# Attention scores over 64-key half-blocks in 32x64 tiles, with a vector-engine mask on the strip that both halves share

## The chip, the cores and the metric

The kernel runs on one core of one Trainium2 chip. Times are device microseconds (us) of that core. Kernels are compared only within the same rounds. The engines are called by the profile's names: PE (TensorE; PEld is its weight load), DVE (VectorE), ACT (ScalarE), POOL (GpSimd) and SP (SyncE).

## The reference, cut to what matters

```python
xn = layernorm(x)                                  # x: 2048 tokens x 512, bf16
qkv = xn @ wqkv                                    # 32 heads of 16
scores = q @ k.T * 16 ** -0.5                      # per head
mask = (i - j >= 0) & (i - j < 256)                # causal, a window of 256 keys
o = softmax(where(mask, scores, -1e9)) @ v
B = ((xn @ w_gate) * (xn @ w_up)) @ w_down         # 512 -> 1792 -> 512, no activation
return x + o @ wo + B
```

The kernel works on four chunks T of 512 tokens. Dense matmuls (projections, gate, up, down, output projection) are "fillers", which it places between the small matmuls of the attention.

## The kernel before

A head pair of one chunk needs, for its 512 queries, keys from 256 tokens back. Before, keys come in blocks of 128. Scores are made transposed (keys on partitions, queries on columns), four heads at a time in four 32-row tiles of PE. A block of 128 keys is met by 384 queries, and of its three 128x128 squares the outer two are triangles that are masked by POOL after the exponential. Three batches of 512 columns hold one parity of the heads:

```python
GROUPS = (                                         # (key block, first q, last q, column)
    ((-2, 0, 0, 0), (0, 0, 2, 128)),
    ((-1, 0, 1, 0), (2, 2, 3, 256)),
    ((1, 1, 3, 0), (3, 3, 3, 384)),
)
def scores(self, T, c, par, i):
    S = self.ps_s.tile([128, 4, 512], F32, tag="S", name="S")
    for kb, q0, q1, col in parts:
        for e in range(4):                         # 4 row tiles, 4 PSUM banks
            nc.tensor.matmul(S[:, e, col:col + n], lhsT=K[32*e: ..., 128 keys],
                             rhs=Q[...], tile_position=(32 * e, 0), ...)      # L223
    nc.scalar.activation(out=P[...], in_=S[...], func=ACT.Exp, scale=0.25)    # L231
    # one affine_select of 128x512 on POOL for each triangle                  # L236, L240
def values(self, T, c, par):                       # two batches later
    for i in range(3):
        for kb, q0, q1, col in self.parts(T, i):
            for e in range(4):                     # 4 column tiles of 17 rows
                nc.tensor.matmul(acc[32*e:32*e+17, ...], lhsT=V[..., 0:17],
                                 rhs=P[:, e, ...], tile_position=(0, 32 * e)) # L256
    # DVE: transpose, reciprocal; then divide(): a product, and a transpose to OT
```

A score batch is one piece of a loop: scores, then (when a pair is complete) the value block of two batches ago, then fillers. `fill` stops at a filler whose `after` has not been reached; the output projection `wo` has one, because it needs OT of its chunk. Three PSUM buffers serve all fillers; DVE empties most of them.

The softmax here doesn't subtract the row's maximum and nothing guards it: scores larger than these inputs give would overflow.

## Time and profile before

| | before |
|---|---|
| time, median of 3 runs (with a fourth, taken later: 279.87) | 279.71 us (279.6 to 280.08) |
| PE, DVE, ACT, POOL busy, of a span of 277.8 us | 269.4, 188.1, 183.1, 164.3 us |
| chain of work that ended last | 89% PE |
| PE instructions in the program | 4830 |

These lines are from the page of the kernel before: part 1 (busy time and share of the span), DVE's row of part 2 (busy tenths in 40 slices of the span), and part 4 (the chain).

```profile
## 1 busy us (share of the span) xinstructions
PE 269.4 (97%) x2396; PEld 115.0 (41%) x2414; DVE 188.1 (68%) x338; ACT 183.1 (66%) x121; POOL 164.3 (59%) x284
...
DVE  6388989788567777858855778774853477777232
...
PE 89%; ACT 5%; DVE 3%; issue 1%; DMA 1%; POOL 0%; ACTq 0%
```

PE is the limit: it is busy for 97% of the span, and the chain is nearly all PE.

The next lines are groups of part 5 (line, engine, operation, output<-input, count | busy us, mean ns of one | idle time before, and what ended it).

```profile
L231 ACT ACTIVATE P<-S 128x2048 bf16<-128x2048 f32 (+2 forms) x96 | 170.0, 1771 | 74.3 <-PE S L223 62.6
L236 POOL TENSOR_SCALAR_AFFINE_SELECT P<-P 128x512 bf16<-128x512 bf16 x128 | 84.7, 662 | 54.3 <-ACT P L231 54.1
...
L256 PE MATMUL accb<-P,V 128*17 128x384 bf16 (+2 forms) x704 | 25.3, 276 | 0.0
```

The exponential (L231) is 96 times up to 1.88 us; POOL's selects (L236 and L240) are 240 times 0.65 us. Both have idle time of tens of us that costs nothing. The 704 score and 704 value matmuls are the PE part of attention.

The timeline of PE near 101 us (start us, duration us, engine, line, operation, and the count that was merged) shows one burst:

```profile
101.36 0.40 PE L223 MATMUL S<-Q,K 16*128 16x256 bf16 x8
101.68 0.83 PE L256 MATMUL accb<-P,V 128*17 128x128 bf16 x24
102.45 0.39 PE L289 MATMUL gp<-xnT,Wg 128*128 128x512 bf16 x1
```

Eight score matmuls take 0.32 us to the start of the next thing, though they have 512 columns in each row tile, and 24 value matmuls take 0.77 us for 1536 columns in each column tile. A 512-column filler matmul starts every 0.216 us, so 1536 columns at full rate are 0.65 us.

### The profile page before, as it was taken

The numbers are of one execution on the slowest core, as the hardware profiler recorded it, in microseconds if no ns is written. First come the engines' busy times: TensorE is split into PE (matmuls) and PEld (weight loads), VectorE is DVE, ScalarE is ACT, GpSimd is POOL, SyncE is SP. The second block draws the span as 40 slices with busy tenths as digits, with TensorE's granted clock in tenths as the row PEclk, the third lists the DMA queues.
The fourth block names the chain that finished last, engine by engine and source line by source line (L and its number), as shares of the span: only waits on it lengthen the run. The fifth ranks groups of instructions, "written<-read, shape, count | busy, mean of one in ns | idle before, by whom it ended". The sixth has DMA issues, their size and how long they took to land.

```text
span 277.8 us, 5829 instructions
## 1 busy us (share of the span) xinstructions
PE 269.4 (97%) x2396; PEld 115.0 (41%) x2414; DVE 188.1 (68%) x338; ACT 183.1 (66%) x121; POOL 164.3 (59%) x284
## 2 busy tenths in 40 slices
PE   7999999999999999999999999999999999999994
PEld 6433433433344434343444344444434444433453
DVE  6388989788567777858855778774853477777232
ACT  3666766786767666688666676769676766767601
POOL 4146666765786656574777656575656566656510
PEclk9999999999999999999999999999999999999999
DMA  6999511000111100000012200000001000000002
GB/s 211 377 371 348 113 21 21 19 2 0 39 40 57 21 2 0 1 2 0 2 40 61 53 2 2 0 2 1 0 2 40 19 21 1 2 0 2 0 2 76
DMA packets 17163, 13.74 MB, mean 49 GB/s; under 512 B 7025, under 2 KB 17137, under 8 KB 17137
## 3 DMA queue, kind: packets, MB, share of 16 engines
q1 hardware_dynamic: 16848, 13.18, 15.6%
q8 instruction: 19, 0.31, 0.5%
q10 hardware_dynamic: 288, 0.20, 0.2%
q14 instruction: 8, 0.06, 0.1%
HBM read 9.70 MB, written 2.10 MB: 42 GB/s over the span
## 4 chain that ended last, share of the span: by engine, by line
PE 89%; ACT 5%; DVE 3%; issue 1%; DMA 1%; POOL 0%; ACTq 0%
PE up L300 18%; PE gp L289 18%; PE psd L317 18%; PE S L223 11%; PE qkp L177 9%; PE accb L256 8%; PE psd L323 5%; ACT P L231 3%; PE vp L165 3%; ACT V L169 1%; DMA x<-in_A_x_dram 1%; DVE st L116 1%; DVE hT L304 0%; DVE gsb L294 0%; PE xTp L151 0%
## 5 line engine op out<-in xcount | busy, mean ns | idle before, releaser
L231 ACT ACTIVATE P<-S 128x2048 bf16<-128x2048 f32 (+2 forms) x96 | 170.0, 1771 | 74.3 <-PE S L223 62.6
L236 POOL TENSOR_SCALAR_AFFINE_SELECT P<-P 128x512 bf16<-128x512 bf16 x128 | 84.7, 662 | 54.3 <-ACT P L231 54.1
L240 POOL TENSOR_SCALAR_AFFINE_SELECT P<-P 128x512 bf16<-128x512 bf16 x112 | 72.5, 647 | 38.4 <-ACT P L231 38.4
L300 PE MATMUL up<-xnT,Wu 128*128 128x512 bf16 x224 | 60.0, 380 | 0.1
L289 PE MATMUL gp<-xnT,Wg 128*128 128x512 bf16 x224 | 59.7, 380 | 0.0
L317 PE MATMUL psd<-Wd,hT 128*128 128x512 bf16 (+1 forms) x225 | 52.3, 366 | 1.4 <-issue 1.1
L263 DVE STREAM_TRANSPOSE at<-accb 128x512 f32<-128x512 f32 x32 | 22.8, 713 | 39.0 <-PE accb L256 39.0
L304 DVE TENSOR_TENSOR hT<-up,gsb 128x512 bf16<-128x512 f32 x56 | 38.1, 680 | 7.8 <-PE up L300 5.8
L294 DVE CAST gsb<-gp 128x512 bf16<-128x512 f32 x56 | 37.9, 676 | 5.9 <-PE gp L289 5.8
L317 PEld LDWEIGHTS <-hT 128*128 128x128 bf16 x238 | 21.5, 98 | 24.9 <-issue 4.7
L289 PEld LDWEIGHTS <-Wg 128*128 128x128 bf16 x224 | 20.0, 98 | 26.1 <-issue 5.2
L177 PE MATMUL qkp<-xnT,Wqkv 128*128 128x512 bf16 x128 | 30.6, 380 | 0.0
L300 PEld LDWEIGHTS <-Wu 128*128 128x128 bf16 x224 | 19.6, 98 | 26.4 <-issue 7.0
L256 PE MATMUL accb<-P,V 128*17 128x384 bf16 (+2 forms) x704 | 25.3, 276 | 0.0
L341 DVE TENSOR_TENSOR y<-psd,x 128x512 bf16<-128x512 f32 (+1 forms) x15 | 9.9, 666 | 17.9 <-PE psd L323 16.5
L223 PE MATMUL S<-Q,K 16*128 16x256 bf16 (+2 forms) x352 | 18.4, 276 | 0.5
L223 PE MATMUL S<-Q,Ko 32*128 32x256 bf16 (+2 forms) x352 | 18.4, 275 | 0.5 <-ACT P L231 0.2
L276 DVE TENSOR_TENSOR on<-at,rz 128x256 bf16<-128x256 f32 x32 | 18.1, 565 | 0.4
L177 PEld LDWEIGHTS <-Wqkv 128*128 128x128 bf16 x128 | 11.4, 98 | 14.6 <-issue 2.7
L256 PEld LDWEIGHTS <-V 128*17 128x17 bf16 x704 | 13.8, 90 | 8.7 <-issue 5.3
L182 DVE CAST K<-qkp 128x512 bf16<-128x512 f32 x16 | 11.0, 688 | 8.9 <-PE qkp L177 8.6
L323 PE MATMUL psd<-Wo,OT 128*128 128x512 bf16 (+1 forms) x67 | 16.6, 367 | 0.2 <-issue 0.2
(39 smaller groups left out, 141.1 us busy)
## 6 DMA issues: line engine op xcount, KB each, us to landing
Wg<-in_B_w_gate_dram SPq DMA_DIRECT2D x2, 896.0 KB, 10.1
Wu<-in_B_w_up_dram SPq DMA_DIRECT2D x2, 896.0 KB, 11.6
Wd<-in_B_w_down_dram SPq DMA_DIRECT2D x1, 1792.0 KB, 15.9
out_dram<-y SPq DMA_DIRECT2D x14, 128.0 KB, 1.7
Wqkv<-in_A_wqkv_dram SPq DMA_DIRECT2D x3, 512.0 KB, 5.5
x<-in_A_x_dram SPq DMA_DIRECT2D x1, 1024.0 KB, 10.5
x<-in_A_x_dram SPq DMA_DIRECT2D x1, 512.0 KB, 10.9
Wo<-in_A_wo_dram SPq DMA_DIRECT2D x1, 512.0 KB, 15.9
```

The costliest lines, as they stand in the source:

```text
L177: nc.tensor.matmul(ps[:], lhsT=self.Wqkv[:, k, lo:lo + 128], rhs=self.xnT[T][:, :, k, :], start=(k == 0), stop=(k == 3))
L223: nc.tensor.matmul(S[:, e, col:col + n], lhsT=(self.Ko if par else self.K)[U][rows, c, 128 * j:128 * j + 128], rhs=self.Q[T][rows, c, 128 ...
L231: nc.scalar.activation(out=P[:, :, lo:hi], in_=S[:, :, lo:hi], func=ACT.Exp, scale=0.25)
L236: nc.gpsimd.affine_select(out=P[:, :, j:j + 128], in_=P[:, :, j:j + 128], pattern=[[0, 4], [1, 128]], compare_op=ALU.is_ge, fill=0.0, base ...
L240: nc.gpsimd.affine_select(out=P[:, :, j:j + 128], in_=P[:, :, j:j + 128], pattern=[[0, 4], [-1, 128]], compare_op=ALU.is_gt, fill=0.0, bas ...
L256: nc.tensor.matmul(acc[32 * e:32 * e + 17, 128 * q0:128 * q0 + n], lhsT=self.V[U][:, v, 8 * c + 2 * e + par, 0:17], rhs=P[:, e, col:col + ...
L289: nc.tensor.matmul(ps[:], lhsT=self.Wg[:, k, 128 * f:128 * f + 128], rhs=self.xnT[T][:, :, k, :], start=(k == 0), stop=(k == 3))
L294: nc.vector.tensor_copy(out=self.gsb[:], in_=ps[:])
L300: nc.tensor.matmul(ps[:], lhsT=self.Wu[:, k, 128 * f:128 * f + 128], rhs=self.xnT[T][:, :, k, :], start=(k == 0), stop=(k == 3))
L304: nc.vector.tensor_tensor(out=self.hT[T][:, f, :], in0=ps[:], in1=self.gsb[:], op=ALU.mult)
L317: nc.tensor.matmul(ps, lhsT=self.hT[T][:, f, 128 * b:128 * b + 128], rhs=self.Wd[:, f, c0:c1], start=(f == 0), stop=False)
L323: self.nc.tensor.matmul(ps, lhsT=self.OT[T][:, c, 128 * b:128 * b + 128], rhs=self.Wo[:, c, c0:c1], start=False, stop=(c == 3))
```

## The change

The intent: cut keys in halves of 64. A half-block is met by 320 queries, not 384, so fewer columns lie outside the window. Score tiles become 32 rows by 64 columns of PE: the two halves of a block sit side by side in the array and give the partitions 0-63 and 64-127 of the same columns. The five batches EVEN, ODD, PLAIN, EVEN, ODD then do for a head pair (both parities) what six did; in the first chunk four do. Of the eight 64-column strips of an EVEN or ODD batch, six need a mask (five in the first chunk; PLAIN needs none). Four (three in the first chunk) are masked by POOL selects of half the old size. The other two are shared: there half 0 and half 1 belong to different key blocks and queries. Their value matmuls read a copy of V in which the other half's rows are zero (Vu, Vl0, Vl1), and their two different masks are put on by DVE, as a minimum with a constant tile. This instruction is placed at the end of the batch, behind its fillers, so that DVE does not stand waiting for the exponential. The pace of the loop changed too: fillers are now shared out evenly over the batches, and no longer by the columns of each batch.

```diff
-        self.work = pool("work", 3)
+        self.work = pool("work", 2)
-        self.ypool = pool("ypool", 5)
+        self.ypool = pool("ypool", 4)
+        self.diag = const.tile([128, 3, 64], BF16, name="diag")          # mask: BIG or 0
...
+    def zero_halves(self, j):
+        for h in (0, 1) if j == 0 else (1,):
+            self.nc.gpsimd.memset(self.Vh[j][h][64 - 64 * h:128 - 64 * h], 0.0)
+    def copy_halves(self, T):
+        for h in range(2):
+            rows = slice(64 * h, 64 * h + 64)
+            self.nc.vector.tensor_copy(out=self.Vh[T % 2][h][rows], in_=self.V[T][rows])
...
+        self.zero_halves(0)                                    # in first_chunk
...
+    def batches(self, T):
+        if T == 0:
+            return [(EVEN, 0), (ODD, 0), (EVEN, 1), (ODD, 1)]
+        return [(EVEN, 0), (ODD, 0), (PLAIN, None), (EVEN, 1), (ODD, 1)]
...
+        return first + second + [                              # of score_pieces: half 0 and 1
+            (par, J, 0, q, 320, 64), (par, J, 1, q + 64, 320, 128),
+            (par, J + 2, 0, q + 256, 128, 384), (par, J + 2, 1, q + 320, 64, 448)]
...
-                nc.tensor.matmul(S[:, e, col:col + n], ... tile_position=(32 * e, 0),
+                nc.tensor.matmul(S[outs, e, col:col + n], ... tile_position=(32 * e, outs.start),
...
-        nc.scalar.activation(out=P[:, :, lo:hi], in_=S[:, :, lo:hi], func=ACT.Exp, scale=0.25)
+        nc.scalar.activation(out=P[:], in_=S[:], func=ACT.Exp, scale=0.25)
...                                                             # selects of 64 columns, 4 per batch
+    def mask_shared(self, T, c, kind, par):
+        if kind == PLAIN:
+            return
+        P = self.strips[(T, c, kind, par)]
+        both = P.rearrange("p e (b x) -> p e b x", x=64)[:, :, 1:7:5, :]
+        m = self.diag[:, 0:2, :] if T == 0 else self.diag[:, 1:3, :]
+        self.nc.vector.tensor_tensor(out=both, in0=both, op=ALU.min,
+                                     in1=m.unsqueeze(1).to_broadcast([128, 4, 2, 64]))
...
+        return first + [(64, 0, J, q, 64), (128, 2, J, q + 64, 256), (384, 1, J, q + 320, 64),
+                        (384, 0, J + 2, q + 256, 64), (448, 2, J + 2, q + 320, 64)]   # value_pieces
...
+            V = self.V[U] if h == 2 else self.Vh[U % 2][h]      # in values
...
             if values(g - LAG):
                 fill(min(spent + 4, upto), g)
                 divide(g - LAG)
+                T, c, par = due[g - LAG]
+                if (c, par) == (3, 1):
+                    self.copy_halves(T + 1)
-            fill(upto, g)
+            if g < len(steps) - 1:
+                fill(upto, g)
+                self.mask_shared(*s)
```

## The prediction

> **What bounds it.** TensorE. Page part 1: PE busy 269.4 of 277.8 us (97%), DVE 188.1, ACT 183.1, POOL 164.3; the chain that ended last is 89% PE; no wait of PE for an engine is over 1.4 us in total (waits). So only PE time counts, unless the change starves PE.
>
> **PE, read from the timeline.** 512-column matmuls start 0.216 us apart. A tiled burst costs its columns plus about 0.1 us of turn-around on each side: one score batch (8 matmuls, 4 row tiles together) runs 101.36-101.68, though 512 columns need 0.213; a value block (24 matmuls, 4 column tiles) 101.68-102.45. In it each piece costs its columns and 3 to 7 ns more.
>
> **Removed.** 96 batches become 76 (12x5 for T>0, 16 for T=0): about 20x0.43 = 8.6 us of PE; ACT 20 fewer exponentials of up to 1.88 us, about -28 us; POOL keeps 240 selects at half the size (about 0.4 us for 0.65, an estimate between the 293 ns at 128 elements and 647 at 512): -60 us. ACT and POOL are off the chain: worth nothing.
>
> **Added.** PE instructions 4830 -> 9438: score matmuls 704 -> 1792, value matmuls 704 -> 1920, each with a weight load. Value columns stay 1536 per head, but in 16 pieces for 6; at 5 ns more each that is +0.05 us x 24, +1.5 us in all. A head pair (T>0) costs now 4x0.43+2x1.19 = 4.1 us, then about 5x0.45+2x0.83 = 3.9 (both 64-key halves side by side, 512 columns): with everything ideal the PE gains only 3 to 4 us, 1.3%.
>
> DVE gains 64 masks (two SBUF inputs, 512 bf16; I estimate 0.45 to 0.65 us from Ko 440 ns and xn 552) and 8 copies of 2304 elements (about 1 us): +35 to 50 us, to 225-240. In gate/up stretches (85-123) DVE is already 76% busy and frees three PSUM buffers; it goes over 90% there, costing PE 1 to 5 us.
>
> **Main doubt: instruction issue.** Now the longest burst is 8+24 matmuls, 64 instructions with loads, in 1.1 us. The new one is 24+64, 176 instructions, with array work for only 1.1 to 1.2 us. The Trainium skill ("TensorE: Matmul & The Clock Gate", table at its head) gives a 64-deep PE queue: today's burst just fits and no gap shows inside it, so the trace does not reveal the sequencer's rate. "Runtime: NRT & Kernel Launch", Instruction fetch mechanics, gives an issue floor of about 20 cycles; at the 1.2 GHz that the TensorE page states that is 17 ns. An estimate from these: 112 unqueued instructions take 1.9 us, 0.7 us over, x24, plus 0.5 x 8 at T=0: about +20 us. At 10 ns it costs nothing; at 28 ns +58.
>
> **Prediction.** -4 (PE work) +2 (DVE) +10 (issue, weighted) = 288 us; range 271 to 320. Faster by over 2% 0.13, within 2% 0.26, slower 0.61.
>
> **What would show it.** ACT about 155 us, POOL near 105, DVE 225-240, mask 0.45-0.65 us. If issue binds: value blocks of 64 matmuls last 1.5 us or more instead of 0.83-0.9, even starts some 15 ns or more per instruction late in the burst, "issue" growing in the waits and the chain; batches alone stay near 0.33 us. If not: value blocks of 0.9 us. If halves do not run side by side, a score batch takes 0.5 us. DVE pressure: PE gp/up waiting for DVE.
>
> **What would make it wrong.** A faster sequencer (then 274-280); column halves sharing one row group serialised (+15 us); DVE masks queued behind POOL selects, delaying PSUM release; shorter turn-arounds than I read.

## The result, and the profile after

The changed kernel took 279.61 us (median of 4 runs, 279.57 to 279.69) against 279.87 us (279.6 to 280.08) for the kernel before. The ratio is 0.9991, with a 95% interval from 0.9977 to 1.0005: the same time. Here and below a ratio is the mean time of one kernel's fast runs over that of the other's of the same rounds, so it is not quite the ratio of the medians quoted. The forecast was 288 us and "slower" at 0.61.

The same lines of the page, after:

```profile
## 1 busy us (share of the span) xinstructions
PE 264.6 (95%) x4697; PEld 128.7 (46%) x4718; DVE 213.7 (77%) x410; ACT 156.4 (56%) x101; POOL 125.1 (45%) x291
...
DVE  6489999959966989885986888885994569888332
...
PE 79%; DVE 13%; issue 2%; ACT 2%; DMA 1%; POOL 1%; DVEq 0%; ACTq 0%
```

PE is 4.8 us less busy and no longer busy for 97%; the chain has 13% of DVE in it where it had 3%. ACT fell by 26.7 us and POOL by 39.2, and no run shows that either bought time, save perhaps in the lead-ins below. The program has 9438 PE instructions.

```profile
L269 ACT ACTIVATE P<-S 128x2048 bf16<-128x2048 f32 x76 | 142.6, 1877 | 98.2 <-PE S L263 74.6
L277 POOL TENSOR_SCALAR_AFFINE_SELECT P<-P 128x256 bf16<-128x256 bf16 x112 | 49.5, 462 | 126.0 <-ACT P L269 126.0
...
L292 DVE TENSOR_TENSOR P<-P,diag 128x512 bf16<-128x512 bf16 x64 | 29.1, 455 | 6.2 <-ACT P L269 6.1
...
L321 PE MATMUL accb<-P,V 128*17 128x64 bf16 (+2 forms) x960 | 26.1, 220 | 0.0
```

There are 76 exponentials for 96. The selects fell from 0.65 to 0.46 us, with half the elements. The mask on DVE costs 0.455 us each, 29.1 us in all.

The timeline of PE for one burst:

```profile
98.49 0.43 PE L263 MATMUL S<-Q,Ko 32*64 32x64 bf16 x24
98.84 0.21 PE L321 MATMUL accb<-P,V 128*17 128x64 bf16 x4
98.88 0.20 PE L321 MATMUL accb<-P,Vl 128*17 128x64 bf16 x4
98.91 0.20 PE L321 MATMUL accb<-P,Vu 128*17 128x64 bf16 x4
...
99.39 0.31 PE L321 MATMUL accb<-P,V 128*17 128x64 bf16 x12
99.63 0.39 PE L364 MATMUL up<-xnT,Wu 128*128 128x512 bf16 x1
```

A score batch of 24 matmuls takes 0.35 us to the first value matmul, and the 64 value matmuls take 0.79 us. Four matmuls of 64 columns, one in each column tile, start every 0.03 us. The whole burst, 88 matmuls and 88 weight loads, takes 1.14 us.

### Where the time of PE went

The trace has every matmul's start. I added up, for all batches, the time from the first score matmul to the first matmul of whatever follows, and the same for value blocks; the lead-in is the median of the time from a filler's last matmul to the first score matmul, less the 0.216 us that the filler's matmul needs.

| PE, us | before | after |
|---|---|---|
| score batches | 96, in all 30.5 | 76, in all 27.7 |
| value blocks | 32, in all 24.8 | 32, in all 26.2 |
| lead-ins, median | 96 x 0.096 = 9.2 | 76 x 0.093 = 7.1 |
| sum | 64.5 | 61.0 |
| lead-ins, added up one by one | 96, in all 10.7 | 76, in all 7.3 |
| sum with these | 66.0 | 61.3 |

So the attention part of PE's program is 3.5 us shorter with the median lead-in, and 4.7 us shorter with every lead-in as it was. The difference lies in the kernel before: nine of its lead-ins take 0.15 to 0.41 us, and for eight of these the profile names the exponential of an earlier batch, which had not yet emptied the only score tile. After the change, one lead-in is that long. The time fell by 0.26 us. So about 4.4 us came back as waits of PE that the kernel before does not have, and the trace shows three places.

First, at the start. These are the lines of the timeline of the changed kernel for DVE's fourth normalisation, and for POOL:

```profile
8.21 2.19 DVE L153 TENSOR_SCALAR xn<-x,mv,rs 128x512 bf16<-128x512 bf16 x1 [0.77 <-POOL rs L145]
8.23 2.01 POOL L119 MEMSET Vu<- 64x2304 bf16 x1
```

In the kernel before, the fourth normalisation is this:

```profile
8.26 0.41 DVE L135 TENSOR_SCALAR xn<-x,mv,rs 128x512 bf16<-128x512 bf16 x1 [0.77 <-POOL rs L127]
```

It took 0.41 us before and 2.19 us after, and it ends at 10.40, just behind the end of POOL's memset (8.23 + 2.01 = 10.24). PE waited for it, 1.6 us by the profile and 1.8 by the starts of its matmuls. In the list of waits of the changed kernel, that is the first line here (the second is about the next place):

```profile
PE xTp L169 <- DVE xn L153: 2.0, 2, 1.6
PE psd L387 <- DVE OT L343: 1.1, 1, 1.1
```

Second, at the end of the first chunk. Here is the chain from a value block (its last matmul started at about 72.36) to the output projection:

```profile
72.63 0.72 DVE L327 STREAM_TRANSPOSE at<-accb 128x512 f32<-128x512 f32 x1 [0.38 <-PE accb L321]
...
73.67 0.42 DVE L340 TENSOR_TENSOR on<-at,rz 128x256 bf16<-128x256 f32 x1
74.13 0.71 DVE L343 STREAM_TRANSPOSE OT<-on 128x512 bf16<-128x512 bf16 x1
...
74.90 0.39 PE L387 MATMUL psd<-Wo,OT 128*128 128x512 bf16 x1 [1.14 <-DVE OT L343]
```

PE sat idle for 1.14 us (1.31 us by the starts of its matmuls), since the next filler in the list was the projection that needs OT, and `fill` does not look behind it.

Third, in the gate and up stretch of the first chunk, where DVE also normalises the next chunk. One of the waits there:

```profile
34.63 0.60 PE L353 MATMUL gp<-xnT,Wg 128*128 128x512 bf16 x2
35.03 0.71 DVE L343 STREAM_TRANSPOSE OT<-on 128x512 bf16<-128x512 bf16 x1
35.67 0.65 DVE L368 TENSOR_TENSOR hT<-up,gsb 128x512 bf16<-128x512 f32 x1
...
36.24 0.39 DVE L153 TENSOR_SCALAR xn<-x,mv,rs 128x512 bf16<-128x512 bf16 x1
36.55 0.42 DVE L292 TENSOR_TENSOR P<-P,diag 128x512 bf16<-128x512 bf16 x1
36.89 0.68 DVE L358 CAST gsb<-gp 128x512 bf16<-128x512 f32 x1
...
37.63 0.59 PE L364 MATMUL up<-xnT,Wu 128*128 128x512 bf16 x2 [0.23 <-DVE gsb L358]
```

The gate matmuls that ended at about 35.2 us (34.63 plus 0.60) were evicted only at 36.89. DVE had the OT transpose, a product, a normalisation and a mask in front of it, and `up`, for which no PSUM buffer was free, started late at 37.63. Between 24 and 52 us DVE is busy for 27.1 of 28 us, against 26.2 before. These are the lines of the view by windows, before and then after (the first busy time is PE's, the third DVE's):

```profile
24.00:52.00 28.00, 27.85 (x231) 10.95 (x224) 26.20 (x52) 18.54 (x13) 18.37 (x33) 1.00 0.35 90
24.00:52.00 28.00, 26.72 (x528) 12.17 (x534) 27.13 (x57) 15.06 (x9) 14.58 (x35) 1.00 0.32 90
```

### The profile page after: what moved, and what is told of

Read it like the earlier page. It is cut to its first block, busy times and chain, and to the rows that moved or that the text cites. A ratio compares the mean times of both kernels' runs of the same rounds, so it can differ in the third digit from the quotient of the medians.

```text
span 277.5 us, 10475 instructions
## 1 busy us (share of the span) xinstructions
PE 264.6 (95%) x4697; PEld 128.7 (46%) x4718; DVE 213.7 (77%) x410; ACT 156.4 (56%) x101; POOL 125.1 (45%) x291
## 4 chain that ended last, share of the span: by engine, by line
PE 79%; DVE 13%; issue 2%; ACT 2%; DMA 1%; POOL 1%; DVEq 0%; ACTq 0%
PE psd L381 17%; PE up L364 15%; PE gp L353 14%; PE qkp L195 11%; PE S L263 9%; PE accb L321 8%; PE psd L387 4%; PE vp L183 3%; DVE gsb L358 2%; DVE hT L368 2%; DVE xn L153 2%; DVE st L134 2%; DVE at L327 1%; ACT P L269 1%; DVE OT L343 1%
## 5 line engine op out<-in xcount | busy, mean ns | idle before, releaser
L269 ACT ACTIVATE P<-S 128x2048 bf16<-128x2048 f32 x76 | 142.6, 1877 | 98.2 <-PE S L263 74.6
L277 POOL TENSOR_SCALAR_AFFINE_SELECT P<-P 128x256 bf16<-128x256 bf16 x112 | 49.5, 462 | 126.0 <-ACT P L269 126.0
L364 PE MATMUL up<-xnT,Wu 128*128 128x512 bf16 x224 | 59.3, 380 | 1.1 <-DVE gsb L358 1.0
L281 POOL TENSOR_SCALAR_AFFINE_SELECT P<-P 128x256 bf16<-128x256 bf16 x128 | 56.0, 460 | 0.0
L381 PE MATMUL psd<-Wd,hT 128*128 128x512 bf16 (+1 forms) x224 | 51.5, 366 | 1.8 <-issue 1.6
L292 DVE TENSOR_TENSOR P<-P,diag 128x512 bf16<-128x512 bf16 x64 | 29.1, 455 | 6.2 <-ACT P L269 6.1
L364 PEld LDWEIGHTS <-Wu 128*128 128x128 bf16 x224 | 20.4, 98 | 25.9 <-issue 2.2
L321 PE MATMUL accb<-P,V 128*17 128x64 bf16 (+2 forms) x960 | 26.1, 220 | 0.0
L321 PE MATMUL accb<-P,Vu 128*17 128x64 bf16 x512 | 20.7, 193 | 0.0
L321 PEld LDWEIGHTS <-V 128*17 128x17 bf16 x960 | 17.1, 92 | 4.9 <-issue 0.4
L321 PE MATMUL accb<-P,Vl 128*17 128x64 bf16 x448 | 18.9, 193 | 0.0
```

What stands on the lines that cost most here:

```text
L269: nc.scalar.activation(out=P[:], in_=S[:], func=ACT.Exp, scale=0.25)
L277: nc.gpsimd.affine_select(out=P[:, :, col:col + 64], in_=P[:, :, col:col + 64], pattern=[[0, 4], [-1, 64]], compare_op=ALU.is_gt, fill=0.0 ...
L281: nc.gpsimd.affine_select(out=P[:, :, col:col + 64], in_=P[:, :, col:col + 64], pattern=[[0, 4], [1, 64]], compare_op=ALU.is_ge, fill=0.0, ...
L292: self.nc.vector.tensor_tensor(out=both, in0=both, op=ALU.min, in1=m.unsqueeze(1).to_broadcast([128, 4, 2, 64]))
L321: nc.tensor.matmul(acc[32 * e:32 * e + 17, q:q + n], lhsT=V[:, v, 8 * c + 2 * e + par, 0:17], rhs=P[:, e, col:col + n], start=(i == 0), st ...
L364: nc.tensor.matmul(ps[:], lhsT=self.Wu[:, k, 128 * f:128 * f + 128], rhs=self.xnT[T][:, :, k, :], start=(k == 0), stop=(k == 3))
```

## The experiments

Eleven more kernels ran. Their ratios to the kernel before have intervals about 0.0013 to each side, except where I give another.

| run | what it is | median us | ratio |
|---|---|---|---|
| the change | | 279.61 | 0.9991 |
| e1_memset_later | memsets after the normalisation | 278.20 | 0.9943 |
| e2_before_memset | kernel before + those memsets | 281.25 | 1.0051 |
| e3_no_mask | the change without DVE masks (wrong result) | 277.94 | 0.9938 |
| e4_pe_only | ... nor memsets nor copies (wrong result) | 276.74 | 0.9887 |
| e5_wo_later | e1 + output projection later | 276.84 | 0.9895 |
| e6_t0_pool_mask | e5 + first chunk's masks on POOL | 277.90 | 0.9929 |
| e7_mask_early | the change, mask right behind its scores | 316.54 | 1.1291 |
| e8_pool_mask | e5 + all masks on POOL | 278.57 | 0.9949 |
| e9_values_32 | the change, value pieces of half the width | 299.21 | 1.0682 |
| e10_gate_on_act | e5 + some gate evictions on ACT | 276.08 | 0.9863 |
| e11_pe_only_wo | e4 + output projection later (wrong result) | 275.45 | 0.9840 |

### e1 and e2: the memsets at the start

```diff
         for b in range(4):
             self.norm_apply(b)
+            last = self.xns[b]
...
+        hold = self.const.tile([128, 1], BF16, name="hold")
+        self.nc.gpsimd.tensor_copy(out=hold[:], in_=last[:, 0:1])
         self.zero_halves(0)
```

> The changed kernel, with the two start-up memsets of zeros on POOL held back (by a one-column POOL copy that reads the last normalised tile) until the fourth normalisation on VectorE is done. Port theory (the memset, 8.23 to 10.24 us, holds something that the normalisation needs, so that it took 2.19 us instead of 0.41 and PE waited 1.81 us at 10.45): that normalisation falls to about 0.41 us and the time falls by 1.8 us, to about 277.8. Rival A (the long normalisation has another cause, the read of the rs tile or of x): it stays 2.19 us and the time 279.6. Rival B (the lost start is caught up later, because another engine than PE bounds the middle): normalisation short, time still 279.6.

Measured: 278.20 us, a ratio of 0.9943. All four normalisations of the start now take about 0.4 us (operations of that line in the first 16 us: minimum, median and maximum ns):

```profile
L153 DVE TENSOR_SCALAR xn<-x,mv,rs x4: 383/414/415, 4.9 to 8.4; 128x512 bf16<-128x512 bf16 x4
```

The counter-test adds two such memsets to the kernel before (`nc.gpsimd.memset` of 64 rows by 2304, behind the last normalisation, with the pool sizes of the change).

> The kernel before, with nothing added but the same two POOL memsets of zeros at the same place (and the pool sizes of the changed kernel, to make room). Port theory: its fourth normalisation grows from 0.41 to about 2.2 us and the time from 279.8 to about 281.6. Rival A: nothing changes, 279.8.

Measured: 281.25 us against 279.96, a ratio of 1.0051, so 1.3 us more, somewhat less than the 1.8 expected. The normalisation grew just as in the change, and PE's next transpose started 1.3 us later than it could:

```profile
8.22 2.19 DVE L136 TENSOR_SCALAR xn<-x,mv,rs 128x512 bf16<-128x512 bf16 x1 [0.77 <-POOL rs L128]
8.25 4.11 POOL L208 MEMSET Vz<- 64x2304 bf16 x2
```

So the memset on POOL, and not something else in the change, makes the normalisation long. The Trainium skill ("SBUF — State Buffer", section "Who interferes with whom") says that DVE and GpSimd share one pair of ports, that `tensor_scalar` on DVE can enter a mode which needs it, and that the pair is held for a whole instruction while "the other fully blocks". In agreement with this, the normalisation's 2.19 us end 0.16 us behind the end of the 2.01 us memset. The two records start too close together (8.21 and 8.23 us) to tell which instruction had the ports first. No run here switched that DVE mode off, so the port is the skill's explanation; the collision itself is measured. The gain passes to the end of the kernel (rival B falls), but it is 1.4 us and not 1.8; the start varies by some tenths between runs.

### e3, e4 and e11: taking DVE's and POOL's new work away

e3 returns from `mask_shared` at once. e4 does that too, leaves out the memsets and copies, and lets each value piece read V itself:

```diff
-            V = self.V[U] if h == 2 else self.Vh[U % 2][h]
+            V = self.V[U]
```

Results are wrong on purpose; PE's program keeps its shapes.

> The changed kernel without the 64 masks on VectorE (wrong result on purpose). Theory (29.1 us of masks on VectorE delay the release of PSUM in the gate/up stretch of the first chunk, where PE waited at 36.4, 37.6, 50.4 us): those waits go, VectorE about 185 us busy, time about 277.6, -2. Rival (VectorE has slack, the masks cost nothing): 279.6.

> The changed kernel with its PE program unchanged in shape, but without the VectorE masks, without the zero memsets and without the copies of V (every value piece reads V itself; wrong result on purpose). Theory (the PE program is 4.7 us shorter, by the sum of its score batches, value blocks and turn-arounds in the trace, and all that was given back to waits for VectorE): about 275.0 us, 1.6 to 1.8% below the kernel before. Rival (the half-block program with twice the instructions is no shorter for PE; the waits only moved): 279 to 279.8.

Measured: 277.94 us without the masks (1.7 less than the change; the matmul starts show that the waits near 36 and 37 us, 0.44 and 0.39 us in the change, are 0.05 and 0.06 here, and the one near 50 us is 0.42 for 0.95) and 276.74 without all three. The theory's 275.0 was missed by 1.7 us. Most of this is the 1.31 us wait at the end of the first chunk: in e4 PE still waits 1.15 us for OT (the line below is from its timeline). With DVE's new work gone it stands there unchanged, so it is no matter of DVE's load. The gains of e1 (1.4) and e3 (1.7) add up to 3.1, and e4 has 2.9: the copies of V, which are 6.3 us of DVE, cost nothing that can be seen.

```profile
72.46 0.39 PE L386 MATMUL psd<-Wo,OT 128*128 128x512 bf16 x1 [1.15 <-DVE OT L342]
```

e11 is e4 with the edit of e5, below.

> The run without masks, memsets and copies (276.7 us), with the later output projection too (wrong result on purpose). Theory (its PE program is 4.7 us shorter than that of before, and the 1.31 us wait was all that it gave back in one piece): about 275.3. Rival (the wait only moves): 276.7.

Measured: 275.45 us, ratio 0.9840, as expected. This is what the half-block PE program is worth when nothing is charged for it: 4.6 us less than the kernel before at 280.01. The table above gives 3.5 us for the work itself and 4.7 us with the longer lead-ins of the kernel before, so it accounts for the whole.

### e5: work between the value block and the projection that needs it

```diff
-                    down(T - 1, b)
+                    down(T - 1, b, 10 if b == 1 else 0)
                     wo(T - 1, b, (0, 1))
+                    if b == 0:
+                        down(T - 1, 1, 0, 10)
                     wo(T - 1, b, (2, 3))
```

> The held-back memsets kept, and five pieces of the next down-projection put before the second half of the first output projection of each chunk. Theory (the 1.31 us wait of PE at the first chunk's end is a dependence: value block, transpose, division, transpose and then the output projection, with no other PE work placed between; it stood in the run without masks and copies too): the wait goes, 276.9 us, 1.3 below the run with the memsets alone. Rival (it is VectorE load, and moves elsewhere): 278.2.

Measured: 276.84 us, as expected, 1.36 us below e1, and the wait is gone from the trace. So this loss was a matter of order. The change did not add the dependence. It moved the fillers against the batches, so that only one matmul of the first down-projection was left behind the value block of the first chunk's last pair; in the kernel before, six still followed that value block.

### e6 and e8: the masks on POOL

```diff
-BIG = 2.0 ** 126
+BIG = 1.0
...
-        self.nc.vector.tensor_tensor(out=both, in0=both, op=ALU.min,
+        eng = self.nc.gpsimd if T == 0 else self.nc.vector      # e8: always gpsimd
+        eng.tensor_tensor(out=both, in0=both, op=ALU.mult,
```

> The same, with the 16 masks of the first chunk alone on POOL (as a product with 0 and 1[...]). Theory (the masks cost time only in the first chunk's gate/up stretch, where the normalisations of the next chunk run too): as much as taking all 64 away, so about 1.3 us less than the run before it, 275.6. Rival 1 (the POOL masks come too late for the value blocks, or hold VectorE's two-port work): same or slower. Rival 2 (the loss is spread over all chunks): 0.4 us less at most.

> The same, with all 64 masks on POOL. POOL 125 us busy now, plus 64 of about 1 us (an estimate from 0.46 us for a select of half the elements): about 190. Theory: VectorE falls to about 185 us, time as with the first chunk's alone, 275.6 (the later chunks lose nothing to masks). Rival: POOL's row of four selects and a mask, about 2.9 us of each 3.6 us batch, delays the values: over 277.

Both misses: 277.90 and 278.57 us, 1.1 and 1.7 us worse than e5. DVE lost the masks of the first chunk in e6, yet its busy time fell only from 212.7 to 211.6 us. The timeline of e6 shows a reason:

```profile
33.09 1.15 POOL L296 TENSOR_TENSOR P<-P,diag 128x512 bf16<-128x512 bf16 x1
33.50 1.02 DVE L344 TENSOR_TENSOR on<-at,rz 128x256 bf16<-128x256 f32 x1
...
35.50 1.15 POOL L296 TENSOR_TENSOR P<-P,diag 128x512 bf16<-128x512 bf16 x1
35.77 1.03 DVE L153 TENSOR_SCALAR xn<-x,mv,rs 128x512 bf16<-128x512 bf16 x1
35.90 1.02 PE L357 MATMUL gp<-xnT,Wg 128*128 128x512 bf16 x4 [0.66 <-DVE hT L372]
```

While a POOL mask of 1.15 us runs, DVE's division (L344) takes 1.02 us, where it took 0.41 without a mask beside it, and the normalisation (L153) 1.03 where it took 0.39, and then PE waits 0.66 us. The work was taken from DVE and given back as blocked time. This looks like the collision at the start: the two DVE instructions end 0.28 and 0.15 us behind the POOL mask, as the normalisation there ended 0.16 us behind the memset. The skill's section names both of its forms: a `tensor_scalar` in a two-port mode, and an instruction with two inputs in SBUF against a GpSimd instruction that reads SBUF (the division has both inputs there). In e8 value blocks also grew, from 26.2 to 27.3 us in all. These runs do not test whether DVE's load matters, because they did not lower it; e3 does.

### e7: the mask at once

```diff
             self.scores(*s)
+            self.mask_shared(*s)
             spent += SCORES
...
                 fill(upto, g)
-                self.mask_shared(*s)
```

> The changed kernel with each mask placed in VectorE's order right behind its score batch instead of behind the batch's other work. Theory (VectorE runs in order and would stand at the mask until the 1.88 us exponential is done, about 2.2 us after the scores, while PE has three PSUM buffers of 0.86 us): PE loses 0.3 to 1 us in each of 64 batches, 300 to 340 us, and the waits name VectorE's mask behind ScalarE's exponential. Rival (the place of the mask does not matter): 279.6.

Measured: 316.54 us, ratio 1.1291 (1.1234 to 1.1348), slower. The waits of this run:

```profile
DVE P L292 <- ACT P L269: 80.0, 51, 3.9
```

DVE waited 80.0 us for the exponential where it waited 6.1 in the change. Putting the mask behind its batch's fillers is worth 37 us.

### e9: where instruction issue does bind

```diff
+        todo = [(P, col + d, h, kb, q + d, n // 2)
+                for P, col, h, kb, q, n in todo for d in (0, n // 2)]
         for i, (P, col, h, kb, q, n) in enumerate(todo):
```

> The changed kernel with every value piece split in two, so that a value block has 128 matmuls and 128 weight loads (most 32 columns wide) for the same columns, and its burst with the scores 304 instructions. It looks for the issue rate that the prediction feared. Theory now (the rate is under 7 ns per instruction, since 112 unqueued ones did not lengthen the 1.18 us burst): pieces of 32 columns need 13 ns of array and up to 8 instructions of some 3 ns, so a value block grows from 0.82 to about 1.0 us if the array's own overhead per piece rules, and to 1.6 us (240 unqueued at 6 to 7 ns) if the rate is just under what the changed kernel used; time plus 6 us to plus 25 us. Rival (17 ns per instruction, as predicted): blocks of 4 us, over 340 us.

Measured: 299.21 us, ratio 1.0682 (1.0656 to 1.0708), slower, inside the range of the theory. One burst of it (here each line merges two pieces of four matmuls):

```profile
105.28 0.43 PE L263 MATMUL S<-Q,Ko 32*64 32x64 bf16 x24
105.64 0.22 PE L322 MATMUL accb<-P,V 128*17 128x32 bf16 x8
105.70 0.21 PE L322 MATMUL accb<-P,Vl 128*17 128x32 bf16 x8
105.75 0.21 PE L322 MATMUL accb<-P,Vu 128*17 128x32 bf16 x8
...
106.13 0.24 PE L322 MATMUL accb<-P,Vl 128*17 128x32 bf16 x8
106.20 0.24 PE L322 MATMUL accb<-P,Vu 128*17 128x32 bf16 x8
...
106.79 0.39 PE L365 MATMUL up<-xnT,Wu 128*128 128x512 bf16 x1
```

Two 32-column pieces take 0.05 us early in the block (105.70 to 105.75), so a group of four matmuls in four column tiles starts every 25 ns; a 64-column group took 29 to 30 ns in the change. The Trainium skill ("TensorE: Matmul & The Clock Gate", Part 1) states that start-to-start "never drops below ≈25 ns however small N is". This agrees with it, if the floor is read per tile: the four tiles of a group start within 10 ns. Below 64 columns, then, narrower pieces buy almost nothing. From the middle of the block on, two pieces take 0.07 us (106.13 to 106.20), 16 instructions at 4.4 ns. That may be the rate at which instructions arrive once the queue has run dry. It is a quarter of the 17 ns that the prediction estimated.

Value blocks are 40.7 us in all here for 26.2 in the change, 14.5 of the 19.6 us more. PE also stopped four times, with 2.5, 2.3, 1.1 and 2.1 us between two matmul starts (from 28.35, 87.24, 140.82 and 193.22 us), and no wait that the profile shows. The second and third stop lie inside value blocks, so the slower pieces account for about 11 of the 14.5 us. The theory had no stops in it, and they make nearly 8 of the 19.6 us; that the time fell inside its range is partly luck. One of the stops, in the timeline:

```profile
195.32 0.82 PE L365 MATMUL up<-xnT,Wu 128*128 128x512 bf16 x3 [1.72 <-issue]
```

In the window around it, 190 to 196 us, the DMA view has one packet of the queue that carries instructions, and this packet began at 192.40 and took 1.44 us. At the other stops such packets began at 28.23, 87.28 and 139.48 us. The page counts 19 such packets before, 37 after and 52 in e9. That PE ran out of fetched instructions there is likely, but no run tests it.

### e10: a version for use

```diff
-        nc.vector.tensor_copy(out=self.gsb[:], in_=ps[:])
+        if T == 0 and f % 3 == 1:
+            nc.scalar.activation(out=self.gsb[:], in_=ps[:], func=ACT.Copy)
+        else:
+            nc.vector.tensor_copy(out=self.gsb[:], in_=ps[:])
```

> The version with the held-back memsets and the later output projection, and every third gate eviction of the first chunk on ScalarE. Theory (what is left of PE's waits in that stretch, about 2 us, is VectorE's load): 0.5 to 1.5 us less than 276.8. Rival (on ScalarE the eviction waits up to 1.9 us behind an exponential and holds a PSUM buffer): same or slower.

Measured: 276.08 us, ratio 0.9863 (0.9850 to 0.9877), a correct result, and 0.76 us below e5. Moving DVE work of the first chunk to ACT helps, where moving it to POOL did not. It is the fastest correct version found and beats both kernels, by 1.4 and about 1.3%. The new order of e5 and these evictions were not tried on the kernel before, so what they would be worth there is not shown.

## Why the prediction was wrong

The failing step is the term "+10 (issue, weighted)" of the sum, and behind it the paragraph "Main doubt: instruction issue", with 17 ns for an instruction and "about +20 us". In its place the runs show that a burst of 176 instructions takes 1.14 us, which is no more than the 1.1 to 1.2 us that the prediction gave to its array work alone.

- **What bounds it: right.** PE, before and after, over the whole span; in the first chunk of the changed kernel DVE is nearly as full (27.1 of 28 us).
- **PE work, "-4": right.** The prediction said 3 to 4 us. The table of the trace gives 3.5, and 4.7 with the longer lead-ins of the kernel before, which the prediction did not count; e11, which charges nothing for it, gives 4.6.
- **Instruction issue, "+10", with up to +58: wrong, none of it shows.** The prediction's own test decides it: "value blocks of 0.9 us" if issue does not bind, "1.5 us or more" if it does. They take 0.79 us, and the burst of 176 instructions 1.14. With a queue of 64, as the skill's TensorE page has it, 112 instructions came in 1.14 us, so one takes at most 10 ns. In e9, 240 come in 1.51 us, at most 6.3 ns each. The figure of about 20 cycles on the page "Runtime: NRT & Kernel Launch" (section "Instruction fetch mechanics") does not hold for this stream of matmuls and weight loads. The trace of before could not tell (its longest burst fits in the queue). The prediction also named "issue" growing in the waits. PE's waits of that name did grow, from 8 to 13, but each is 0.16 us long and stands before the first down- or output-projection matmul behind a tiled burst, none inside a burst. So the prediction gave its largest weight to a figure that nothing measured supported, and turned an even case into a forecast of slower. Its own list of what would make it wrong has the case that came: "A faster sequencer (then 274-280)".
- **DVE, "+35 to 50 us" of work and "+2" of time: busy time too high, loss right in size but not in place.** The masks are 29.1 us at 0.455 each and the copies 6.3, together at the low end of the range. DVE's busy time rose by only 25.6 us to 213.7, not to 225-240. In part that is because records of DVE overlap: added up one by one, they rose by 32.7 us. The division fell from 18.1 to 15.0 us, because POOL's shorter selects collide with it less often; that is my reading. The traces agree with it (the 17 divisions over 0.6 us in the kernel before all begin while a select runs and end about 0.27 us behind it; after, there are five), but no run tests it. Without the masks the time is 1.7 us less (e3), so that +2 came close is partly luck. It was lost where the prediction had not looked, in the first chunk, where DVE was already full; from 85 to 123 us, which it named, DVE went from 76 to 83% only, and PE was as busy as before (37.7 us for 37.6).
- **Left out: two items of 1.4 us each.** The memsets on POOL hold up a DVE operation at the start (e1: 1.4 us), and a change of pace puts an output projection right behind the division that it needs (e5: 1.4 us). The prediction costed each engine's added work, but not two engines meeting, nor the new order.
- **Column halves in one row group run side by side: right.** A score batch of 512 columns per half takes 0.35 to 0.36 us. Serial halves would need 1024 columns, 0.43 us, before any turn-around.
- **ACT "about 155": right (156.4). POOL "near 105": 125.1**: the selects, added up one by one, fell by 46.5 us (157.2 to 110.7), not 60, since one of half the elements is 0.46 us and not 0.4, and the three memsets, which it forgot, are 6.1.

Put together: -4.7 of PE's program with its lead-ins, +1.7 for masks, +1.4 for memsets, +1.4 for the order. The sum is -0.2, against a measured -0.26. The large change moved nothing because a gain of 1.6% on the bounding engine was given back in three waits of that engine, none of which is in the attention part itself.

## What to carry to other kernels

On an engine that is busy for 97%, look at the waits that a change creates for it in other places, at the start, at phase changes and where a second engine is already full: three short ones can pay back the whole gain, and each has its own cheap cure. Work moved to POOL is not free for DVE; ask which DVE instruction will run beside it. And when a forecast rests on a rate that the trace of before cannot show, give the term little weight, or say plainly that it decides the sign.

## What the Trainium skill lacked or had wrong

- "Runtime: NRT & Kernel Launch", section "Instruction fetch mechanics": an issue floor of about 20 cycles per instruction, 17 ns at 1.2 GHz. PE took 112 instructions beyond its queue in 1.14 us (at most 10 ns each), and 240 in 1.51 us (at most 6.3 ns) in e9. The page should say that it does not hold for matmuls and weight loads. The skill itself does not lack this: "TensorE: Matmul & The Clock Gate", Part 1, says that these two go straight to the engine and do not use the sequencer (NX) whose floor it is, which the prediction overlooked.
- "TensorE: Matmul & The Clock Gate", Part 3: it does not give the cost of the turn from full-array matmuls to tiled ones. Here the lead-in is 0.096 us for each burst, 9.2 us in the kernel before.
- "TensorE: Matmul & The Clock Gate", Part 1: the floor of 25 ns agrees (25 ns for 32 columns, 29 for 64), but the page doesn't say that it counts per tile, with four tiles starting within 10 ns.
- "SBUF — State Buffer", section "Who interferes with whom": agrees in kind (0.41 to 2.19 us beside a memset, 0.41 to 1.02 us for a two-input DVE product beside a POOL product). It gives no way to see the collision in a profile, where the blocked DVE instruction only looks long and no wait is recorded for it.
